# Windowed attention into a rational feed-forward layer on one Trainium2 core: chunks of 512 tokens, the division by remainder, and no GpSimd in the loop

## The chip, the cores and the metric

The program runs on one core of one Trainium2 chip. The core has a matrix engine (TensorE, PE in the profile, with its weight loads listed apart as PEld), VectorE (DVE), ScalarE (ACT), GpSimd (POOL), a queue that issues transfers (SyncE, SP), and 16 DMA engines. Operands lie in SBUF; matmuls write to PSUM, eight banks of 512 float32 columns on each of 128 partitions. The metric is the device time of one execution in microseconds, lower is better.

## The reference

Attention over 8 batches and 8 heads of 576 positions and 64 dimensions, each position seeing itself and the 63 before it; then a feed-forward layer on all 4608 tokens of width 512, with a rational function between its two matrices (512 x 2048 and 2048 x 512).

```python
scores = scale * np.matmul(q, k.transpose(0, 1, 3, 2))
rel = pos[:, None] - pos[None, :]
scores = np.where((rel >= 0) & (rel < 64), scores, -1000000000.0)
attn = np.exp(scores - np.max(scores, axis=-1, keepdims=True))
attn = attn / (np.sum(attn, axis=-1, keepdims=True) + 1e-09)
attn_out = np.matmul(attn, v)
x = attn_out.transpose(0, 2, 1, 3).reshape(B * S, H * D)
h = x @ w_in
P = a[0] + a[1] * h + a[2] * h**2 + a[3] * h**3
Q = 1.0 + np.abs(b[0]) * np.abs(h) + np.abs(b[1]) * h**2
out = (P / (Q + 1e-6)) @ w_out
```

The two weight matrices are handed over as 64-bit floats; the others as 32-bit.

## The kernel before

The tokens are cut into chunks of `CH` = 384. For each chunk the attention is computed in four **units**, one for each pair of heads (`hp`); a unit yields one 128 x 384 block of x, stored transposed as a rounded part `xh` and a remainder `xl`. The feed-forward layer then runs in **steps** (c, i): chunk c and block i of the 16 blocks of 128 hidden columns.

A step has three parts. `ffn1` (L234) makes one PSUM bank h of 128 hidden columns by 384 tokens with 12 matmuls: for each of four 128-row blocks of x the products of high weight and low x, high and high, low weight and high x. Then comes the **gate**, P divided by Q: ScalarE takes |h| and the first linear form of P; VectorE finishes P but for a[0]; the denominator is formed in `u`, for the first `DEC` = 28 gates by ScalarE (L250) and VectorE (L251), for the other 164 by GpSimd (L253, L254); ScalarE makes the reciprocal as exp(-ln u); VectorE improves it by one Newton step (L258, L259), multiplies (L260), ScalarE rounds the result to `gh` (L263) and VectorE takes the remainder `gl` (L264). `ffn2` (L274) adds the step's share of the output with 9 matmuls, three for each of the three 128-token tiles, into PSUM banks that stay open for the chunk's 16 steps. ffn2 of a step is written `LAG` = 3 steps behind its ffn1.

The order of steps: the first half of chunk 0 (8 steps), all 16 of chunk 1, the second half of chunk 0, and then chunk by chunk. So each weight block is decoded once and used soon after. The output of chunk 0's first half is kept in SBUF (`part`) and added at its end.

Weight decoding (`decode`, L101) turns 512 x 128 64-bit floats into two float32 parts. A transfer fills `w_st`; ScalarE takes the magnitude of the upper words, VectorE limits it, shifts it and merges in three bits of the lower word and the sign (L114 to L118); ScalarE rounds to the high part (L121), VectorE subtracts for the low part (L122). There are 32 decodings, all of them within the first 32 steps.

An attention unit has four parts. `unit_load` (L142) issues q, k and v; where a batch ends inside the chunk each of these is issued twice. `unit_scores` (L172): per 64-position tile and head one matmul of 64 x 128 scores into a PSUM tile of two banks; VectorE scales and masks (L188, L192) and takes the maximum; ScalarE exponentiates and sums; VectorE divides, from chunk 2 on GpSimd multiplies by the reciprocal sum (L205). `unit_transpose` (L208) transposes on TensorE into the same two-bank buffer and ScalarE copies out. `unit_av` (L217) multiplies by v into a third bank and ScalarE and VectorE store `xh`, `xl`. The units of the next chunk are spread over the steps before it, one every four steps, `AHEAD` = 3 steps early.

PSUM: two banks for h, two for scores and transposes, one for av, three for the output. Scratch tiles of the gate have two buffers each, `gh` and `gl` LAG + 1. The framework sets the semaphores, and orders each engine's instructions by its own estimate of their times; each engine then works its list in order, SP its transfers.

Of the kernel before, what the change touches and what calls it, by code (L numbers as in the profile page):

```python
# [31 lines left out]
def swa_rational_ffn(ctx: ExitStack, tc: tile.TileContext, qT, kT, v, w_in, w_out, a, b, out):  # L32
    nc = tc.nc
    P = 128
    B, HP, _, S = qT.shape
# [57 lines left out]

    wi_h = const.tile([P, NCC, DFF], F32R, name="wi_h")
    wi_l = const.tile([P, NCC, DFF], F32R, name="wi_l")
# [2 lines left out]
    w_in_v = w_in.rearrange("(cc p) f -> p cc f", p=P)
    w_out_v = w_out.rearrange("(fc p) e -> p fc e", p=P)

    def decode(src, hi, lo):  # L101

        w = stage.tile([P, 512, 2], U32, name="w_st", bufs=2)
        if len(src.shape) == 3:
            nc.sync.dma_start(out=w.rearrange("p (c n) two -> p c (n two)", c=src.shape[1]), in_=src)
        else:
            nc.sync.dma_start(out=w.rearrange("p n two -> p (n two)"), in_=src)
        low, high = w[:, :, 0], w[:, :, 1]
        c = stage.tile([P, 512], U32, name="w_c")
        cf = c.bitcast(F32)  # L110


        nc.scalar.activation(cf, w.bitcast(F32)[:, :, 1], AF.Abs)
        nc.vector.tensor_scalar(out=cf, in0=cf, scalar1=2.0 ** -15, scalar2=None, op0=ALU.max)  # L114
# [3 lines left out]
        nc.vector.scalar_tensor_tensor(out=c, in0=high, scalar=0xC0000000, in1=c, op0=ALU.bitwise_and, op1=ALU.bitwise_or)  # L118
        if len(hi.shape) == 3:
            cf = cf.rearrange("p (c n) -> p c n", c=hi.shape[1])  # L120
        nc.scalar.copy(out=hi, in_=cf)  # L121
        nc.vector.tensor_tensor(out=lo, in0=cf, in1=hi.bitcast(F32), op=ALU.subtract)  # L122
# [10 lines left out]

    def segments(c):

        g, left = c * TC, TC
        while left:
            n = min(left, TPB - g % TPB)
            yield g // TPB, g % TPB, n
            g, left = g + n, left - n  # L140

    def unit_load(c, hp):  # L142
# [3 lines left out]
        row = v.shape[2]  # L146
        kw, vw, first = [], [], None
        j = kb = vb = 0
        for bi, t0, n in segments(c):
            nc.sync.dma_start(out=q[:, j:j + n, :].rearrange("p t s -> p (t s)"),  # L150
                              in_=qT[bi, hp, :, t0 * WIN:(t0 + n) * WIN])
            k0 = max(t0 - 1, 0)
            nw = n if t0 else n - 1
            nc.sync.dma_start(out=kt[:, kb:kb + nw + 1, :].rearrange("p t s -> p (t s)"),
                              in_=kT[bi, hp, :, k0 * WIN:(k0 + nw + 1) * WIN])
            nc.sync.dma_start(out=vt[:, vb:vb + nw, :],
                              in_=bass.AP(v.tensor, (bi * S + k0 * WIN) * row + hp * P,
                                          [[row, P], [WIN * row, nw], [1, P]]))
            for t in range(t0, t0 + n):
                if t == 0:  # L160
                    first = j
                w = max(t - 1, 0) - k0
                kw.append(kb + w)
                vw.append(vb + w)
                j += 1
            kb += nw + 1
            vb += nw
# [225 lines left out]
```

## Time and profile before

| | |
|---|---|
| median of 3 runs | 1039.95 us |
| lowest run | 1039.42 us |
| span of the profiled execution | 1038.0 us |
| TensorE busy | 954.8 us, 92% |
| VectorE busy | 896.2 us, 86% |
| ScalarE busy | 706.8 us, 68% |
| GpSimd busy | 383.4 us, 37% |
| moved by DMA | 64.08 MB, 62 GB/s |

The three runs are 1039.42, 3231.52 and 1039.95 us; the second is an outlier that the median leaves out. The span runs from the first instruction of the profiled execution to its last and lies 2.0 us under the median; the page gives no other time for that execution.

How to read it: the busy shares of two engines are close, so the totals don't say which one sets the time. They are averages over stretches in which different work goes on, and have to be taken apart by time. A matmul's listed duration includes its run through the array and overlaps the next one's; the pace of TensorE is the distance between starts.

### The profile page before, as it was taken

How to read it: one execution, taken by the hardware profiler on the slowest of the kernel's cores; microseconds unless marked ns; L12 is line 12 of the kernel's file. 1: busy time of each engine (PE TensorE's matmuls, PEld its weight loads, DVE VectorE, ACT ScalarE, POOL GpSimd, SP SyncE). 2: the span in 40 equal slices, each digit the busy share in tenths (PEclk: the TensorE clock that was granted, in tenths of full speed). 3: DMA queues.
4: the chain of work that ended last, by engine and by line, in shares of the span. 5: the costliest groups of instructions: out<-in, count | busy, mean ns of one | idle time of the engine just before them, and what ended most of it. 6: DMA issues, size and time to landing. Idle time of an engine off the chain costs nothing.

```text
span 1038.0 us, 18200 instructions
## 1 busy us (share of the span) xinstructions
PE 954.8 (92%) x6624; PEld 839.2 (81%) x6624; DVE 896.2 (86%) x1639; ACT 706.8 (68%) x1762; POOL 383.4 (37%) x395
## 2 busy tenths in 40 slices
PE   2677686999999999999999999999999999999997
PEld 2566565789888889888888888888888898888996
DVE  5999899988888888888888888888888888888885
ACT  4687767677676666666676676766766766766664
POOL 2000002004554543543543544544544444445332
PEclk9889789999999999999999999999999999999999
DMA  6744433121111111111112112111112112100000
GB/s 188 203 124 129 125 105 92 41 72 32 59 43 47 60 49 46 64 40 48 59 33 57 60 30 64 64 31 57 59 30 60 60 31 64 63 16 2 31 1 30
DMA packets 68536, 64.08 MB, mean 62 GB/s; under 512 B 4448, under 2 KB 61792, under 8 KB 68448
## 3 DMA queue, kind: packets, MB, share of 16 engines
q1 hardware_dynamic: 68448, 62.93, 19.8%
q8 instruction: 52, 0.85, 0.4%
q14 instruction: 36, 0.29, 0.1%
HBM read 53.48 MB, written 9.44 MB: 61 GB/s over the span
## 4 chain that ended last, share of the span: by engine, by line
DVE 33%; PE 22%; ACT 20%; POOL 16%; issue 5%; DMA 3%; POOLq 0%; SPq 0%; DVEq 0%; ACTq 0%
PE o L284 11%; PE h L239 9%; ACT sm L201 8%; POOL u L253 6%; DVE u L258 6%; POOL u L254 5%; POOL sm L205 5%; DVE nmx L198 4%; DVE u L259 3%; DVE gl L264 3%; DMA w_st<-w_in 3%; DVE num L247 2%; ACT ah L256 2%; DVE num L260 2%; DVE num L246 2%
## 5 line engine op out<-in xcount | busy, mean ns | idle before, releaser
L239 PE MATMUL h<-xl,wi_h 128*128 128x384 f32 x768 | 266.4, 347 | 24.6 <-DVE num L247 18.0
L239 PE MATMUL h<-xh,wi_h 128*128 128x384 f32 x768 | 261.5, 341 | 0.0
L239 PE MATMUL h<-xh,wi_l 128*128 128x384 f32 x768 | 260.8, 340 | 0.0
L284 PE MATMUL o<-wo_h,gl 128*128 128x512 f32 x576 | 236.7, 411 | 25.4 <-DVE gl L264 25.3
L253 POOL TENSOR_SCALAR u<-ah,b_sb 128x384 f32<-128x384 f32 x164 | 134.8, 825 | 284.2 <-ACT ah L244 172.4
L284 PE MATMUL o<-wo_h,gh 128*128 128x512 f32 x576 | 229.4, 398 | 0.0
L284 PE MATMUL o<-wo_l,gh 128*128 128x512 f32 x576 | 228.4, 397 | 0.0
L205 POOL TENSOR_TENSOR sm<-sm,rs 128x768 f32<-128x768 f32 x40 | 72.6, 1814 | 347.0 <-DVE rs L204 202.1
L264 DVE TENSOR_TENSOR gl<-num,gh 128x384 fp32r<-128x384 f32 x192 | 165.1, 864 | 15.0 <-ACT gh L263 11.9
L201 ACT ACTIVATE sm<-sm,nmx 128x128 f32<-128x128 f32 x288 | 111.8, 390 | 94.4 <-DVE nmx L198 94.2
L254 POOL TENSOR_TENSOR u<-u,ah 128x384 f32<-128x384 f32 x164 | 171.6, 1053 | 8.3
L239 PEld LDWEIGHTS h<-xl,wi_h 128*128 128x128 f32 x768 | 146.5, 191 | 33.1 <-DVE num L247 20.9
L284 PEld LDWEIGHTS o<-wo_h,gl 128*128 128x128 f32 x576 | 110.1, 191 | 57.9 <-DVE gl L264 32.1
L245 ACT ACTIVATE num<-h,a_sb 128x384 f32<-128x384 f32 x192 | 128.7, 670 | 35.3 <-DVE gl L264 35.2
L239 PEld LDWEIGHTS h<-xh,wi_h 128*128 128x128 f32 x768 | 146.6, 191 | 4.5
L256 ACT ACTIVATE ah<-u 128x384 f32<-128x384 f32 x192 | 100.3, 522 | 72.3 <-POOL u L254 70.4
L239 PEld LDWEIGHTS h<-xh,wi_l 128*128 128x128 f32 x768 | 146.5, 191 | 0.0
L258 DVE SCALAR_TENSOR_TENSOR u<-u,ah 128x384 f32<-128x384 f32 x192 | 111.1, 579 | 36.0 <-ACT ah L257 35.8
L284 PEld LDWEIGHTS o<-wo_h,gh 128*128 128x128 f32 x576 | 110.1, 191 | 24.9
L284 PEld LDWEIGHTS o<-wo_l,gh 128*128 128x128 f32 x576 | 110.3, 191 | 19.5
L246 DVE TENSOR_TENSOR num<-num,h 128x384 f32<-128x384 f32 x192 | 105.0, 547 | 21.9 <-ACT num L245 21.8
L263 ACT CAST gh<-num 128x384 fp32r<-128x384 f32 x192 | 96.7, 508 | 36.6 <-DVE num L260 36.6
(47 smaller groups left out, 1239.8 us busy)
## 6 DMA issues: line engine op xcount, KB each, us to landing
out<-ob SPq DMA_DIRECT2D x33, 256.0 KB, 2.0
w_st<-w_in SPq DMA_DIRECT2D x16, 512.0 KB, 4.1
w_st<-w_out SPq DMA_DIRECT2D x16, 512.0 KB, 3.7
q<-qT SPq DMA_DIRECT2D x32, 192.0 KB, 3.2
vt<-v SPq DMA_DIRECT2D x16, 384.0 KB, 3.4
vt<-v SPq DMA_DIRECT2D x16, 320.0 KB, 3.5
kt<-kT SPq DMA_DIRECT2D x16, 224.0 KB, 3.6
kt<-kT SPq DMA_DIRECT2D x16, 192.0 KB, 3.4
```

The costliest lines, as they stand in the source:

```text
L201: nc.scalar.activation(sm[:, j, :], sm[:, j, :], AF.Exp, bias=nmx[:, j:j + 1], accum_out=sums[:, j:j + 1])
L205: (nc.vector if c < 2 else nc.gpsimd).tensor_tensor(out=sm, in0=sm, in1=rs.unsqueeze(2).broadcast_to([P, NR, P]), op=ALU.mult)
L239: nc.tensor.matmul(h, w[:, cc, i * P:(i + 1) * P], x[c, cc], start=n == 0, stop=n == 3 * NCC - 1)
L245: nc.scalar.activation(num, h, AF.Identity, scale=a_sb[:, 3:4], bias=a_sb[:, 2:3])
L246: nc.vector.tensor_tensor(out=num, in0=num, in1=h, op=ALU.mult)
L253: nc.gpsimd.tensor_scalar(out=u, in0=ah, scalar1=b_sb[:, 1:2], scalar2=b_sb[:, 0:1], op0=ALU.mult, op1=ALU.add)
L254: nc.gpsimd.tensor_tensor(out=u, in0=u, in1=ah, op=ALU.mult)
L256: nc.scalar.activation(ah, u, AF.Ln, bias=QADD)
L258: nc.vector.scalar_tensor_tensor(out=u, in0=u, scalar=QADD, in1=ah, op0=ALU.add, op1=ALU.mult)
L263: nc.scalar.copy(out=gh, in_=num)
L264: nc.vector.tensor_tensor(out=gl, in0=num, in1=gh.bitcast(F32), op=ALU.subtract)
L284: nc.tensor.matmul(acc[c][t], g[:, ts], w[:, i, :], start=first and n == 0, stop=last and n == 2)
```

## The change

Tokens: `CH` = 512, nine chunks instead of twelve, the steps 144 instead of 192, four output tiles instead of three, 12 matmuls in `ffn2`. The inputs are laid out over all batches in a row, so that a unit's q, k and v are one transfer each (in chunk 0 the first k and v tile come apart). Where a batch begins inside a chunk, the mask is one for all tiles and the tile's older half is overwritten by a memset.

Attention uses single banks: two buffers of one bank serve scores, transposes and av. The transposed tiles pass the output buffers' ring (`ob`, two slots).

The gate no longer uses GpSimd. It has no Newton step: with r = exp(-ln Q) the high part is the rounded P r, the remainder is (P - Q gh) r.

Decoding works in place in `w_st`, with one VectorE operation less; ScalarE scales the upper word by 2^-112 instead of taking its magnitude. The weight arrays are laid out by block.

`LAG` is 2. Chunk 0's partial sum goes to DRAM and comes back.

```diff
-CH = 384
+CH = 512
-DEC = 28
-LAG = 3
+LAG = 2
...
+    dram = ctx.enter_context(tc.tile_pool(name="dram", bufs=1, space=bass.MemoryType.DRAM))
-    ps_a = ctx.enter_context(tc.tile_pool(name="ps_a", bufs=3, space=bass.MemoryType.PSUM))
+    ps_a = ctx.enter_context(tc.tile_pool(name="ps_a", bufs=2, space=bass.MemoryType.PSUM))
...
-        nc.scalar.activation(cf, w.bitcast(F32)[:, :, 1], AF.Abs)
-        nc.vector.tensor_scalar(out=cf, in0=cf, scalar1=2.0 ** -15, scalar2=None, op0=ALU.max)
-        nc.vector.tensor_scalar(out=c, in0=c, scalar1=3, scalar2=0x3FFFFFF8, op0=ALU.logical_shift_left, op1=ALU.bitwise_and)
-        nc.vector.scalar_tensor_tensor(out=c, in0=low, scalar=29, in1=c, op0=ALU.logical_shift_right, op1=ALU.bitwise_or)
-        nc.vector.scalar_tensor_tensor(out=c, in0=high, scalar=0xC0000000, in1=c, op0=ALU.bitwise_and, op1=ALU.bitwise_or)
-        nc.scalar.copy(out=hi, in_=cf)
-        nc.vector.tensor_tensor(out=lo, in0=cf, in1=hi.bitcast(F32), op=ALU.subtract)
+        w = stage.tile([P, 1024], F32, name="w_st")
+        nc.sync.dma_start(out=w.bitcast(U32), in_=src)
+        w = w.rearrange("p (n two) -> p n two", two=2)
+        wu = w.bitcast(U32)
+        low, high = wu[:, :, 0], wu[:, :, 1]
+        nc.scalar.activation(w[:, :, 1], w[:, :, 1], AF.Copy, scale=2.0 ** -112)
+        nc.vector.tensor_scalar(out=low, in0=low, scalar1=29, scalar2=None, op0=ALU.logical_shift_right)
+        nc.vector.scalar_tensor_tensor(out=low, in0=high, scalar=0x80000000, in1=low, op0=ALU.bitwise_and, op1=ALU.bitwise_or)
+        nc.vector.scalar_tensor_tensor(out=low, in0=high, scalar=3, in1=low, op0=ALU.logical_shift_left, op1=ALU.bitwise_or)
+        c = w[:, :, 0]
+        nc.scalar.copy(out=hi, in_=c)
+        nc.vector.tensor_tensor(out=lo, in0=c, in1=hi.bitcast(F32), op=ALU.subtract)
...
+        nc.sync.dma_start(out=q.rearrange("p t s -> p (t s)"), in_=qT[hp, :, g * WIN:(g + TC) * WIN])
+        lo = 0 if g else 1
+        if lo:
+            nc.sync.dma_start(out=kt[:, 0, :], in_=kT[hp, :, 0:WIN])
+            for e in range(2):
+                nc.sync.dma_start(out=vt[e * 64:e * 64 + 64, 0, :], in_=v[0:WIN, hp * P:(hp + 1) * P])
+        nc.sync.dma_start(out=kt[:, lo:, :].rearrange("p t s -> p (t s)"), in_=kT[hp, :, (g + lo - 1) * WIN:(g + TC) * WIN])
+        nc.sync.dma_start(out=vt[:, lo:, :], in_=bass.AP(v.tensor, (g + lo - 1) * WIN * row + hp * P,
+                                                          [[row, P], [WIN * row, TC - lo], [1, P]]))
...
+        ps = [bank(), bank()]
...
+            nc.vector.scalar_tensor_tensor(out=sm[:, z * PR:(z + 1) * PR, :], in0=ps[z].rearrange("p (r c) -> p r c", c=P),
+                                           scalar=SCALE, in1=mask.unsqueeze(1).broadcast_to([P, PR, P]), op0=ALU.mult, op1=ALU.min)
+        for j in u["first"]:
+            e = j % 2
+            nc.vector.memset(sm.rearrange("p (z r) c -> p z r c", z=2)[e * 64:e * 64 + 64, :, j // 2, 0:WIN], NEG)
...
-        (nc.vector if c < 2 else nc.gpsimd).tensor_tensor(out=sm, in0=sm, in1=rs.unsqueeze(2).broadcast_to([P, NR, P]), op=ALU.mult)
+        nc.vector.tensor_tensor(out=sm, in0=sm, in1=rs.unsqueeze(2).broadcast_to([P, NR, P]), op=ALU.mult)
...
+        for z in range(2):
+            pT = op.tile([P, CH], F32, name="pT", tag="ob")
+            ps = bank()
+            for p in range(PR):
+                nc.tensor.transpose(ps[:, p * P:(p + 1) * P], u["sm"][:, z * PR + p, :], ident)
+            nc.scalar.copy(out=pT, in_=ps)
...
-        n_gates[0] += 1
-        if n_gates[0] <= DEC:
-            nc.scalar.activation(u, ah, AF.Identity, scale=b_sb[:, 1:2], bias=b_sb[:, 0:1])
-            nc.vector.tensor_tensor(out=u, in0=u, in1=ah, op=ALU.mult)
-        else:
-            nc.gpsimd.tensor_scalar(out=u, in0=ah, scalar1=b_sb[:, 1:2], scalar2=b_sb[:, 0:1], op0=ALU.mult, op1=ALU.add)
-            nc.gpsimd.tensor_tensor(out=u, in0=u, in1=ah, op=ALU.mult)
-        nc.scalar.activation(ah, u, AF.Ln, bias=QADD)
-        nc.scalar.activation(ah, ah, AF.Exp, scale=-1.0)
-        nc.vector.scalar_tensor_tensor(out=u, in0=u, scalar=QADD, in1=ah, op0=ALU.add, op1=ALU.mult)
-        nc.vector.scalar_tensor_tensor(out=u, in0=u, scalar=2.0, in1=ah, op0=ALU.subtract, op1=ALU.mult, reverse0=True)
-        nc.vector.scalar_tensor_tensor(out=num, in0=num, scalar=a_sb[:, 0:1], in1=u, op0=ALU.add, op1=ALU.mult)
-        nc.scalar.copy(out=gh, in_=num)
-        nc.vector.tensor_tensor(out=gl, in0=num, in1=gh.bitcast(F32), op=ALU.subtract)
+        nc.scalar.activation(u, r, AF.Identity, scale=b_sb[:, 1:2], bias=b_sb[:, 0:1])
+        nc.vector.tensor_tensor(out=u, in0=u, in1=r, op=ALU.mult)
+        nc.scalar.activation(r, u, AF.Ln, bias=QADD)
+        nc.scalar.activation(r, r, AF.Exp, scale=-1.0)
+        nc.vector.scalar_tensor_tensor(out=gh, in0=num, scalar=a_sb[:, 0:1], in1=r, op0=ALU.add, op1=ALU.mult)
+        nc.vector.scalar_tensor_tensor(out=u, in0=u, scalar=QADD, in1=gh.bitcast(F32), op0=ALU.add, op1=ALU.mult)
+        nc.vector.scalar_tensor_tensor(out=u, in0=num, scalar=a_sb[:, 0:1], in1=u, op0=ALU.add, op1=ALU.subtract)
+        nc.vector.tensor_tensor(out=gl, in0=u, in1=r, op=ALU.mult)
...
-            part[c] = const.tile([P, NTS, DO], F32, name="part")
+            part[c] = dram.tile([NTS, P, DO], F32, name="part")
             for t in range(NTS):
-                nc.scalar.copy(out=part[c][:, t, :], in_=o[t])
+                ob = op.tile([P, DO], F32, name="ob", tag="ob")
+                nc.scalar.copy(out=ob, in_=o[t])
+                nc.sync.dma_start(out=part[c][t], in_=ob)
...
+            pool, tag = (op, "ob") if s < total - 1 or t < 2 else (tmp, ("r", "u")[t - 2])
+            ob = pool.tile([P, DO], F32, name="ob", tag=tag)
             if c in part:
-                nc.vector.tensor_tensor(out=ob, in0=o[t], in1=part[c][:, t, :], op=ALU.add)
+                nc.sync.dma_start(out=ob, in_=part[c][t])
+                nc.vector.tensor_tensor(out=ob, in0=o[t], in1=ob, op=ALU.add)
...
+        if k >= 2:
+            unit_av(0, k - 2)
         if 1 <= k <= NU:
             unit_transpose(0, k - 1)
-        if k >= 2:
-            unit_av(0, k - 2)
```

More of the change, by code (lines that the diff above doesn't have):

```diff
@@ L91, in swa_rational_ffn @@
     make_identity(nc, ident)
[L94 to L95 removed]
+    wi_h = const.tile([P, NF, NCC, P], F32R, name="wi_h")
+    wi_l = const.tile([P, NF, NCC, P], F32R, name="wi_l")
     wo_h = const.tile([P, NF, DO], F32R, name="wo_h")
     wo_l = const.tile([P, NF, DO], F32R, name="wo_l")
[L98 to L99 removed]
     def decode(src, hi, lo):
[L103 to L122 removed]
@@ L124, in load_w_in @@
+        nc.vector.scalar_tensor_tensor(out=low, in0=high, scalar=3, in1=low, op0=ALU.logical_shift_left, op1=ALU.bitwise_or)
+        c = w[:, :, 0]
+        nc.scalar.copy(out=hi, in_=c)
+        nc.vector.tensor_tensor(out=lo, in0=c, in1=hi.bitcast(F32), op=ALU.subtract)
     def load_w_in(i):
-        sl = slice(i * P, (i + 1) * P)
-        decode(w_in_v[:, :, 2 * i * P:2 * (i + 1) * P], wi_h[:, :, sl], wi_l[:, :, sl])
+        f = "p c n -> p (c n)"
+        decode(w_in[i], wi_h[:, i].rearrange(f), wi_l[:, i].rearrange(f))
@@ L128, in load_w_out @@
     def load_w_out(i):
-        decode(w_out_v[:, i, :], wo_h[:, i, :], wo_l[:, i, :])
+        decode(w_out[i], wo_h[:, i, :], wo_l[:, i, :])
     xh, xl = {}, {}
     live = {}
[L134 to L140, printed above, removed]
     def unit_load(c, hp):
@@ L145, in unit_load, with bank @@
         vt = kv.tile([P, TC, P], F32, name="vt")
[L146 to L167, printed above, removed]
-        m0 = None if first is None else MASKS[first]
-        live[c, hp] = dict(q=q, kt=kt, vt=vt, kw=kw, vw=vw, m0=m0)
+        row = v.shape[1]
+        g = c * TC
+        nc.sync.dma_start(out=q.rearrange("p t s -> p (t s)"), in_=qT[hp, :, g * WIN:(g + TC) * WIN])
[7 more added lines that the diff above has]
+                                                          [[row, P], [WIN * row, TC - lo], [1, P]]))
+        live[c, hp] = dict(q=q, kt=kt, vt=vt, first=[j for j in range(TC) if (g + j) % TPB == 0])
+    def bank():
+        return ps_a.tile([P, 512], F32, name="ps", tag="ps")
     def unit_scores(c, hp):
         u = live[c, hp]
-        ps = ps_a.tile([P, 2, 512], F32, name="ps_s", bufs=1)
+        ps = [bank(), bank()]
         for p in range(PR):
@@ L209, in unit_transpose @@
         u = live[c, hp]
-        ps = ps_a.tile([P, 2, 512], F32, name="ps_s", bufs=1)
-        for j in range(2 * PR):
-            nc.tensor.transpose(ps[:, j // PR, (j % PR) * P:(j % PR + 1) * P], u["sm"][:, j, :], ident)
-        pT = att.tile([P, 2, PR * P], F32, name="pT", bufs=1)
-        nc.scalar.copy(out=pT, in_=ps[:, :, 0:PR * P])
-        u["pT"] = pT
+        u["pT"] = []
+        for z in range(2):
[4 more added lines that the diff above has]
+            nc.scalar.copy(out=pT, in_=ps)
+            u["pT"].append(pT)
     def unit_av(c, hp):
         u = live.pop((c, hp))
-        ps = ps_a.tile([P, TC, WIN], F32, name="ps_x", bufs=1)
+        ps = bank()
         for j in range(TC):
             for z in range(2):
-                nc.tensor.matmul(ps[z * 64:z * 64 + 64, j, :], u["vt"][:, u["vw"][j], z * 64:z * 64 + 64],
-                                 u["pT"][:, z, j * WIN:(j + 1) * WIN], start=True, stop=True)
+                nc.tensor.matmul(ps[z * 64:z * 64 + 64, j * WIN:(j + 1) * WIN], u["vt"][:, j, z * 64:z * 64 + 64],
+                                 u["pT"][z][:, j * WIN:(j + 1) * WIN], start=True, stop=True)
         xh[c, hp] = xp.tile([P, CH], F32R, name=f"xh{hp}")
         xl[c, hp] = xp.tile([P, CH], F32R, name=f"xl{hp}")
-        x = ps.rearrange("p t s -> p (t s)")
-        nc.scalar.copy(out=xh[c, hp], in_=x)
-        nc.vector.tensor_tensor(out=xl[c, hp], in0=x, in1=xh[c, hp].bitcast(F32), op=ALU.subtract)
+        nc.scalar.copy(out=xh[c, hp], in_=ps)
+        nc.vector.tensor_tensor(out=xl[c, hp], in0=ps, in1=xh[c, hp].bitcast(F32), op=ALU.subtract)
     gs = {}
-    n_gates = [0]
     def ffn1(c, i):
```

70 lines of the change are left out of this document (28 added, 42 removed).

## The prediction

> **What bounds the kernel now.** I read the row of slices on the page first, then windows over the two stages that it shows, then the timeline of each stage's busiest engine. Two slice rows:
>
> ```profile
> PE   2677686999999999999999999999999999999997
> DVE  5999899988888888888888888888888888888885
> ```
>
> A slice is 26 us. TensorE is full from the eighth on, VectorE before that. Windows make it exact (columns: length, then busy time of PE, weight loads, VectorE, ScalarE, GpSimd):
>
> ```profile
> 0.00:252.66 252.66, 187.23 (x1318) 157.75 (x1319) 228.47 (x455) 175.18 (x426) 24.43 (x39) 0.91 0.38 113
> 20.00:200.00 180.00, 130.49 (x913) 109.34 (x914) 171.25 (x345) 125.95 (x308) 8.38 (x3) 0.88 0.42 124
> 60.00:100.00 40.00, 33.80 (x252) 28.05 (x251) 40.00 (x85) 30.65 (x72) 0.00 (x0) 0.91 0.43 128
> 200.00:252.66 52.66, 52.11 (x353) 44.90 (x352) 47.20 (x91) 40.21 (x89) 9.17 (x9) 1.00 0.15 47
> 357.00:971.00 614.00, 603.90 (x4291) 536.47 (x4292) 529.54 (x937) 423.64 (x1077) 287.87 (x283) 1.00 0.15 47
> ```
>
> So there are two stages. The **head** (weight decoding, the 32 steps of chunks 0 and 1) is VectorE's: 171.25 of 180 us, and all of 60 to 100. The **steady part** is TensorE's: 603.90 of 614. At 252.66 the 33rd step starts, and I cut there. TensorE's timeline gives its beat:
>
> ```profile
> 252.66 0.34 PE L239 MATMUL h<-xl,wi_h 128*128 128x384 f32 x1
> ...
> 282.80 0.38 PE L212 MATMUL ps_s<-ident,sm 128*128 128x128 f32 x2
> ...
> 301.97 0.49 PE L212 MATMUL ps_s<-ident,sm 128*128 128x128 f32 x3
> ...
> 357.04 0.50 PE L284 MATMUL o<-wo_h,gl 128*128 128x512 f32 x1 [1.50 <-DVE gl L264]
> ...
> 959.39 0.34 PE L239 MATMUL h<-xl,wi_h 128*128 128x384 f32 x1
> ...
> 988.56 0.40 PE L284 MATMUL o<-wo_h,gl 128*128 128x512 f32 x1
> ...
> 992.70 0.34 PE L239 MATMUL h<-xl,wi_h 128*128 128x384 f32 x1
> ...
> 996.88 0.40 PE L284 MATMUL o<-wo_h,gl 128*128 128x512 f32 x1
> ...
> 1033.99 0.40 PE L284 MATMUL o<-wo_h,gh 128*128 128x512 f32 x1
> ```
>
> 988.56 to 992.70 holds 18 matmuls of 512 columns, 0.230 us each; from there to 996.88 are 24 of 384, 0.174 each. A step is 12 x 0.174 + 9 x 0.230 = 4.16. Four steps with one attention unit take 301.97 - 282.80 = 19.17, so a unit costs TensorE 19.17 - 16.64 = 2.53. A chunk takes (959.39 - 252.66) / 9 = 78.53, of which 16 x 4.16 + 4 x 2.53 = 76.7 is work and 1.5 the wait at the chunk's edge (357.04).
>
> VectorE's beat in the saturated stretch: instructions start closer together than they last.
>
> ```profile
> 65.97 0.96 DVE L205 TENSOR_TENSOR sm<-sm,rs 128x768 f32<-128x768 f32 x1
> 66.84 0.43 DVE L114 TENSOR_SCALAR w_c<-w_c 128x512 f32<-128x512 f32 x1
> 67.18 0.56 DVE L264 TENSOR_TENSOR gl<-num,gh 128x384 fp32r<-128x384 f32 x1
> 67.65 0.56 DVE L251 TENSOR_TENSOR u<-u,ah 128x384 f32<-128x384 f32 x1
> ...
> 72.05 0.70 DVE L118 SCALAR_TENSOR_TENSOR w_c<-w_st,w_c 128x512 uint32<-128x512 uint32 x1
> 72.65 0.62 DVE L247 SCALAR_TENSOR_TENSOR num<-num,a_sb,h 128x384 f32<-128x384 f32 x1
> 73.17 0.57 DVE L258 SCALAR_TENSOR_TENSOR u<-u,ah 128x384 f32<-128x384 f32 x1
> ```
>
> I take spacings as prices: 0.87 for 768 elements, 0.34 for the one-input form on 512, 0.47 for two inputs on 384, 0.60 on 512, 0.52 with a coefficient column on 384. So 128 elements more cost 0.13, and the coefficient form on 512 is 0.65, the multiply on 1024 elements 1.13. Other rows, less the same 0.09:
>
> ```profile
> L264 DVE TENSOR_TENSOR gl<-num,gh 128x384 fp32r<-128x384 f32 x192 | 165.1, 864 | 15.0 <-ACT gh L263 11.9
> L198 DVE TENSOR_REDUCE nmx<-sm 128x6 f32<-128x768 f32 x48 | 45.4, 947 | 0.0
> L203 DVE TENSOR_SCALAR sums<-sums 128x6 f32<-128x6 f32 x48 | 8.2, 171 | 31.6 <-ACT sm L201 31.6
> L192 DVE SCALAR_TENSOR_TENSOR sm<-ps_s,mask 128x384 f32<-128x384 f32 x64 | 32.5, 550 | 0.0
> L205 POOL TENSOR_TENSOR sm<-sm,rs 128x768 f32<-128x768 f32 x40 | 72.6, 1814 | 347.0 <-DVE rs L204 202.1
> ```
>
> L264 averages 0.86 against 0.56 in the stretch where GpSimd was idle (0.00 above). That surcharge goes with GpSimd; TensorE hides it today.
>
> **The change, part by part.**
>
> *Chunks of 512, TensorE.* Steps fall from 192 to 144, each 24 x 0.230 = 5.52. All FFN matmuls: 192 x 4.16 = 799 before, 144 x 5.52 = 795 after. Units fall from 48 to 36, each 4/3 of 2.53 = 3.37: unchanged in sum. A chunk: 16 x 5.52 + 4 x 3.37 + 1.5 = 103.3, where 512 tokens cost 78.53 x 4/3 = 104.7 before. The gain is 1.4 per chunk.
>
> *VectorE per gate.* Seven operations, four at 0.60 and three at 0.65: 4.35 for 512 tokens, against 5 x 0.47 + 2 x 0.52 = 3.39 for 384 while GpSimd had no part. Per unit: two masks 1.20, maximum 1.12, two small ones of L203's form 0.18, multiply 1.13 (GpSimd's before, from chunk 2 on), xl 0.60, and 32 memsets over 36 units: 4.3. A memset is bounded by 0.08 (L203's form) and 0.47; it is tiny, so 0.1. Before: 2 x 0.46 + 0.86 + 0.18 + 0.87 + 0.47 = 3.3. A steady chunk then asks 16 x 4.35 + 4 x 4.3 = 87 us of VectorE under 103.3 of TensorE: 84%, hidden if dependent operations are interleaved as now. If each ran at its whole duration plus the 0.02 between, it would be about 99: still under.
>
> *Decoding.* One operation less: 0.34 + 3 x 0.60 = 2.14 against 2 x 0.34 + 3 x 0.60 = 2.48. The shift now reads and writes every second word, which no row shows; bounds 0.34 and 0.60, and I take 0.34, the row of the same form. The two-input forms read such a stride already in L118. The Trainium skill, VectorE: DVE Perf Modes, "What auto-detection actually checks", names no unit stride for the fast one-source form of 32-bit data; by it the shift stays short, and no run here shows it.
>
> *The head.* Up to the cut VectorE does 32 decodings, 31 gates, 12 units. Before: 79.4 + 105.1 + 39.6, less what GpSimd took, 4.9: 219. After: 68.5 + 134.9 + 51.6 = 255. The 36 more, at the 95% busy of 20 to 200, move the cut by 38 to 291. Between 200 and 252.66 VectorE had 5.5 idle, so 285 is the low end; a long shift adds 32 x 0.26 / 0.95 = 9. TensorE's work up to there, 61 halves of a step at 2.76 and 12 units at 3.37, is 209 and stays below.
>
> *ScalarE.* It gains the denominator's scaling (from GpSimd) and loses the cast of gh.
>
> ```profile
> L244 ACT ACTIVATE ah<-h 128x384 f32<-128x384 f32 x192 | 93.2, 485 | 35.6 <-PE h L239 33.2 <-DVE u L259 1.4 <-PE ps_s L212 0.8
> L245 ACT ACTIVATE num<-h,a_sb 128x384 f32<-128x384 f32 x192 | 128.7, 670 | 35.3 <-DVE gl L264 35.2
> L250 ACT ACTIVATE u<-ah,b_sb 128x384 f32<-128x384 f32 x28 | 19.7, 708 | 0.0
> L256 ACT ACTIVATE ah<-u 128x384 f32<-128x384 f32 x192 | 100.3, 522 | 72.3 <-POOL u L254 70.4 <-DVE u L251 1.5
> L257 ACT ACTIVATE ah<-ah 128x384 f32<-128x384 f32 x192 | 101.1, 527 | 3.8
> L201 ACT ACTIVATE sm<-sm,nmx 128x128 f32<-128x128 f32 x288 | 111.8, 390 | 94.4 <-DVE nmx L198 94.2
> L228 ACT CAST xh<-ps_x 128x384 fp32r<-128x384 f32 x48 | 22.4, 468 | 2.8 <-PE ps_x L223 2.8
> L298 ACT COPY ob<-o 128x512 f32<-128x512 f32 x30 | 17.4, 580 | 2.7 <-PE o L284 1.4 <-DMA out<-ob 1.3
> ```
>
> 128 elements add 0.11 (L298 against L228): 0.60 + 0.78 + 0.82 + 0.63 + 0.64 = 3.5 a step, with exponentials and copies under 5 of 6.4: hidden.
>
> *Slack of a gate (LAG 2).* Its chain: 3.5 on ScalarE, 0.69 + 0.75 + 0.69 + 0.75 + 0.69 on VectorE, some 0.5 of hand-overs: 7.5. Between ffn1 and its ffn2 TensorE has four halves, 11.0, so 3.5 are left. Before, LAG 3 gave six halves of 2.08: 12.5 for shorter instructions. The wait at the edge (357.04) is of this kind; I keep its 1.5 per chunk, bounds 0 and 1.5 + 2.8 (rival 2). Behind a late ffn2 TensorE's whole queue stands, the next ffn1 first.
>
> *DMA and SP.*
>
> ```profile
> out<-ob SPq DMA_DIRECT2D x33, 256.0 KB, 2.0
> w_st<-w_in SPq DMA_DIRECT2D x16, 512.0 KB, 4.1
> w_st<-w_out SPq DMA_DIRECT2D x16, 512.0 KB, 3.7
> SPq L156 <- PE ps_x L223: 510.5, 44, 19.3
> ```
>
> Unit loads shrink from four issues to three; SP idles 510.5 us behind the v loads, so this is worth 0. The weights' new layout makes w_in like w_out, 0.4 sooner, under VectorE's queue. Chunk 0's partial sum goes to DRAM and back: four stores and four loads join SP's queue, loads and copies behind them. At step 33 each of two slots passes load, add, store (2.0 + 0.7 + 2.0) before its second use; the next chunk's ffn2 waits between 0 and 5, and I take 2. Masks (16 selects fewer on GpSimd), av ahead of the transposes in the prologue: 0, since the first weights' landing covers them.
>
> *Sum.* Last chunk and end: before 1033.99 + 0.40 - 959.39 = 75.0, of which 66.6 beat and 8.4 drain; after 88.3 + 8.7 = 97. From the last matmul to the span's end 3.6. So 291 + 2 + 6 x 103.3 + 97 + 3.6 = 1013.4, against the span of 1038.0; the median lies 2.0 above that span, so 1015.4, called **1016**, 2.3% under the median. Its own range is 1003 to 1030.
>
> **The rivals.**
> 1. *Slower: attention eats the gate's slack.* At each unit VectorE takes 4.3 us (2.4 before, the multiply being GpSimd's) and ScalarE eight exponentials of 0.39, in front of a gate with 3.5 to spare; if both fall into one chain, 3.9 are lost. With 24 units after the cut that is 1016 + 94 = 1110. It decides from 1.9 a unit on (45 us). For it: the edge already waits on gl. Against: VectorE's 16% idle lets the gate catch up.
> 2. *The two-slot ring and single banks.* Four output copies and each unit's two transposed tiles pass the same two slots; the third copy waits for a landing of 2.0. At most 2.8 at the edge and 0.7 (a copy) per unit: 5.6 x 7 = 39; half of it gives 1036.
> 3. *The head is heavier.* The long shift adds 9, and staging tiles held to the last subtraction, 1.3 longer, starve a decoding: up to 32 x 1.3 / 2 = 21. Middle: 1033.
> 4. *No overlap on VectorE.* Every operation of 255 us in the head pays its duration, 0.09 more on some 440 instructions: 40 us, 1056. Against: starts 67.18 and 67.65 with 0.56 each. The Trainium skill, same page, "The DRAIN you can't avoid", says that the next operation cannot issue before the pipe is empty; by that rule this is the time, and the trace does not bear it out.
> 5. *Better:* no wait at the edges, the head at 285: 1016 - 10 - 8 = 998.
>
> **How the numbers follow.** Forecast 0.52, two thirds of it under 1019; rivals 1 to 5: 0.12, 0.14, 0.12, 0.03, 0.07. Two per cent, 20.8 us, is about what this measurement tells apart. Faster: 0.35 + 0.07 = 0.42. Slower: 0.12. Same: 0.46. Range 1002 to 1052: it leaves out rival 1 and some 0.07 of rivals 4 and 5.
>
> **What would show it.** The 33rd step near 291 with VectorE full before; 512-column matmuls in L239's place 0.230 apart; chunks of 103 to 104; VectorE near 85 to 90% busy, with no instruction stretched; the shift at 0.43. Wrong if TensorE waits for gl or h more than once a chunk, if chunks pass 107, or the cut lies past 305.

## The result, and the profile after

The changed kernel takes 1058.18 us (median of 4 runs, 1057.24 to 1058.55) against 1039.68 for the kernel before (a fourth run of it took 1038.65): a ratio of 1.0176, interval 1.0160 to 1.0191. It is slower, though by less than 2%, where 1016 us and a gain of 2.3% were forecast, and it lies 6 us above the range. The profiled execution spans 1056.3 us, 42.9 more than the 1013.4 of the forecast's sum.

The page of the changed kernel, its busy times and the slices (26 us each):

```profile
PE 985.2 (93%) x6048; PEld 786.5 (74%) x6048; DVE 903.3 (86%) x1424; ACT 675.0 (64%) x1506; POOL 2.1 (0%) x11
...
PE   2769768899998999999999999999999999999998
...
DVE  5789968999887988888888888888889888888886
...
PEclk9899978999999999999999999999999999999999
```

TensorE is full from the ninth slice on, but for the thirteenth. In the first eight, VectorE, which was to be full there, is at 9 only three times. Windows, the first from the start of the span to step 33, the others cut at the first feed-forward matmul of steps 1, 17, 33, 41 and 113 (columns: length, then busy time of PE, weight loads, VectorE, ScalarE, GpSimd, then PEclk, DMA share, GB/s):

```profile
0.00:308.76 308.76, 248.58 (x1576) 194.74 (x1577) 264.16 (x440) 198.29 (x458) 2.07 (x11) 0.93 0.35 109
...
36.02:209.35 173.33, 136.32 (x928) 104.22 (x926) 152.35 (x263) 116.55 (x277) 0.00 (x0) 0.88 0.43 135
209.35:308.76 99.41, 98.82 (x509) 79.14 (x508) 88.59 (x138) 64.45 (x128) 0.00 (x0) 1.00 0.09 28
308.76:369.46 60.70, 55.03 (x391) 43.55 (x390) 50.94 (x81) 33.51 (x78) 0.00 (x0) 1.00 0.29 87
369.46:848.89 479.43, 479.43 (x3026) 385.52 (x3024) 417.80 (x649) 315.58 (x718) 0.00 (x0) 1.00 0.16 51
```

The same two halves of the head in the kernel before:

```profile
29.30:171.13 141.83, 103.19 (x750) 85.79 (x750) 135.45 (x273) 104.02 (x263) 3.18 (x2) 0.86 0.45 133
171.13:252.66 81.53, 74.87 (x460) 64.79 (x461) 74.75 (x147) 57.80 (x125) 14.37 (x10) 0.98 0.16 50
```

Three places hold nearly all of the 42.9 us.

- **The head**: the 33rd step starts at 308.76 instead of 291, +17.8. Its second half (steps 17 to 32) is TensorE's: 98.82 busy of 99.41 us. In the first half neither engine is full: VectorE idles 21.0 of 173.33 us, in the kernel before 6.4 of 141.83.
- **The eight steps from the 33rd**: 60.70 us, of which TensorE is idle 5.7, where eight steady steps take 479.43 / 9 = 53.27. That is +7.4; 2 were allowed for.
- **The steady part**: 106.5 us a chunk (16 steps) instead of 103.3, with no idle TensorE at all; six chunks make +19.4.

The rest is small: up to step 129 the remaining steps give back 2.2, and the last chunk with the end takes 103.1 instead of 100.6. Sum: 17.8 + 5.4 + 19.4 - 2.2 + 2.5 = 42.9.

In the steady part one row of TensorE's timeline shows where it goes. The unit that runs there (columns: start, length, then the instruction and its count):

```profile
490.87 1.15 PE L182 MATMUL ps<-pT,vt 128*64 128x64 f32 x32
491.95 1.09 PE L145 MATMUL ps<-kt,q 64*64 64x128 f32 x16
...
498.91 1.09 PE L145 MATMUL ps<-kt,q 64*64 64x128 f32 x16
```

and the kernel before:

```profile
386.26 0.89 PE L182 MATMUL ps_s<-kt,q 64*64 64x128 f32 x24
```

Before, a unit's 24 score instructions (two for each matmul) stood together, the two heads in turn, and took 0.89 us. Now there are 32 in two groups, one for each head, 7 us apart, and **each group of 16 takes 1.09 us, as long as 32 in alternation do** (1.10, e1 below). Four instructions start every 0.109 us while the heads alternate, two with one head alone. The Trainium skill, TensorE: Matmul & The Clock Gate, "The mechanism" (Part 3), says that matmuls on different parts of the array overlap; the trace agrees (32 in 1.10 us), and adds that the two heads' matmuls overlap only where they stand next to each other in the queue (16 alone take 1.09).

The groups of the changed kernel (columns: count, then busy time and mean ns) that answer to the prediction's prices:

```profile
L145 PE MATMUL ps<-kt,q 64*64 64x128 f32 x1152 | 79.5, 291 | 13.4 <-DMA kt<-kT 6.1 <-DVE sm L149 4.5 <-DVE xl L187 1.6
...
L99 DVE TENSOR_SCALAR w_st<-w_st 128x512 uint32<-128x512 uint32 x32 | 13.5, 423 | 26.1 <-DMA w_st<-w_in 17.3 <-DMA w_st<-w_out 8.4
...
L216 DVE TENSOR_TENSOR gl<-u,r 128x512 fp32r<-128x512 f32 x144 | 98.6, 685 | 1.2
```

The strided shift stayed short (0.423), and with GpSimd out of the loop gl averages 0.685 (L216), close to the 0.69 that the prediction's chain has for it. Scores are busy for 79.5 us; before it was 47.0 for as many instructions.

### The profile page after: what moved, and what is told of

It reads as the page before. It is cut to its first block, busy times and chain, and to the rows that moved or that the text cites. A ratio compares the mean times of both kernels' runs of the same rounds, so it can differ in the third digit from the quotient of the medians.

```text
span 1056.3 us, 15824 instructions
## 1 busy us (share of the span) xinstructions
PE 985.2 (93%) x6048; PEld 786.5 (74%) x6048; DVE 903.3 (86%) x1424; ACT 675.0 (64%) x1506; POOL 2.1 (0%) x11
## 4 chain that ended last, share of the span: by engine, by line
PE 79%; DVE 11%; DMA 6%; ACT 3%; SPq 1%; issue 1%; ACTq 0%; DVEq 0%
PE o L236 35%; PE h L196 34%; PE ps L145 5%; DMA w_st<-w_in 4%; PE ps L182 3%; PE ps L173 2%; DMA w_st<-w_out 2%; ACT sm L159 1%; DVE w_st L100 1%; DVE w_st L101 1%; DVE gh L213 1%; DVE nmx L156 1%; DVE wi_l L104 1%; DVE num L206 1%; DVE u L208 1%
## 5 line engine op out<-in xcount | busy, mean ns | idle before, releaser
L196 PE MATMUL h<-xl,wi_h 128*128 128x512 f32 x576 | 235.1, 408 | 14.1 <-DVE num L207 11.4
L196 PE MATMUL h<-xh,wi_h 128*128 128x512 f32 x576 | 231.7, 402 | 0.0
L196 PE MATMUL h<-xh,wi_l 128*128 128x512 f32 x576 | 230.5, 400 | 0.0
L206 DVE TENSOR_TENSOR num<-num,h 128x512 f32<-128x512 f32 x144 | 98.5, 684 | 39.1 <-ACT num L204 38.0
L205 ACT ACTIVATE u<-r,b_sb 128x512 f32<-128x512 f32 x144 | 117.5, 816 | 0.0
L204 ACT ACTIVATE num<-h,a_sb 128x512 f32<-128x512 f32 x144 | 111.8, 776 | 0.0
L213 DVE SCALAR_TENSOR_TENSOR gh<-num,a_sb,r 128x512 fp32r<-128x512 f32 x144 | 107.3, 746 | 2.8 <-ACT r L211 2.6
L215 DVE SCALAR_TENSOR_TENSOR u<-num,a_sb,u 128x512 f32<-128x512 f32 x144 | 107.5, 747 | 1.4
L207 DVE SCALAR_TENSOR_TENSOR num<-num,a_sb,h 128x512 f32<-128x512 f32 x144 | 106.8, 741 | 0.5
L208 DVE TENSOR_TENSOR u<-u,r 128x512 f32<-128x512 f32 x144 | 98.8, 686 | 3.1 <-ACT u L205 2.3
```

The costliest lines, as they stand in the source:

```text
L196: nc.tensor.matmul(h, w[:, i, cc, :], x[c, cc], start=n == 0, stop=n == 3 * NCC - 1)
L204: nc.scalar.activation(num, h, AF.Identity, scale=a_sb[:, 3:4], bias=a_sb[:, 2:3])
L205: nc.scalar.activation(u, r, AF.Identity, scale=b_sb[:, 1:2], bias=b_sb[:, 0:1])
L206: nc.vector.tensor_tensor(out=num, in0=num, in1=h, op=ALU.mult)
L207: nc.vector.scalar_tensor_tensor(out=num, in0=num, scalar=a_sb[:, 1:2], in1=h, op0=ALU.add, op1=ALU.mult)
L208: nc.vector.tensor_tensor(out=u, in0=u, in1=r, op=ALU.mult)
```

## The experiments

Each was compared with the kernel before on the same chip; intervals are 95%. "Steps 33 to 40" stands for the eight steps from the 33rd.

### Are separated heads the steady loss?

**e1_two_bank_tile.** One PSUM tile of two banks instead of two single ones, so that both heads' scores can only run together.

```diff
-    def bank():
-        return ps_a.tile([P, 512], F32, name="ps", tag="ps")
+    def banks():
+        t = ps_a.tile([P, 2, 512], F32, name="ps", tag="ps", bufs=1)
+        return t[:, 0, :], t[:, 1, :]
```

> The changed kernel with one PSUM tile of two banks for scores, transposes and av in place of two single banks; all else as in it. Theory A (TensorE does the scores of the two heads one after the other, because the second bank is not yet free when the first is): a unit's 32 score instructions stand together again and take about 1.1 us instead of 2 x 1.02, a steady chunk falls from 106.5 to 102.7 us, and the time falls by 24 units x 0.95 plus a little in the head, to 1030 to 1036 us. Rival B (the unit is longer for another reason: more switches, longer drains of 512 columns): chunk and time stay within 3 us of 1058. Rival C (one slot of two banks holds transposes and av up): TensorE waits inside chunks, 1058 or more.

1140.70 us, ratio 1.0978 (1.0961 to 1.0996). Its TensorE timeline (in brackets the idle time before, and what ended it):

```profile
583.19 1.10 PE L146 MATMUL ps<-kt,q 64*64 64x128 f32 x32 [1.41 <-DVE xl L189]
...
589.06 0.80 PE L198 MATMUL h<-xl,wi_h 128*128 128x512 f32 x1 [3.18 <-DVE num L209]
...
600.22 1.15 PE L184 MATMUL ps<-pT,vt 128*64 128x64 f32 x32 [2.19 <-ACT pT L176]
```

Together, 32 instructions take 1.10: the price is confirmed. But with one slot the scores wait for the subtraction that reads x, av waits for the copy of the transposed tiles, and TensorE stands still: the other way of losing time was far dearer.

**e2_before_heads_in_turn.** The kernel before, with the loop over heads outside.

```diff
-        for p in range(PR):
-            for z in range(2):
+        for z in range(2):
+            for p in range(PR):
```

> The kernel before, with the score matmuls of one head issued ahead of those of the other; nothing else. Theory A: its 24 score instructions of a unit take 24 x 0.064 = 1.5 us instead of 0.82, a chunk 81.3 instead of 78.5, and with 36 units behind the cut the time rises by about 26 us, to 1063 to 1070. Rival B: within 3 us of 1040.

1044.18 us, ratio 1.0046 (1.0029 to 1.0062). The unit's group:

```profile
389.41 1.15 PE L182 MATMUL ps_s<-kt,q 64*64 64x128 f32 x24
```

1.15 instead of 0.89: the effect is there in the kernel before too, but well under the size expected (0.26 us a unit instead of 0.7, and 4.8 us in all instead of 26). In this group the starts of the single instructions show the second head's first matmuls between the first head's last ones; nothing else stands between the heads there. In the changed kernel seven us of other work do.

**e5_scores_together.** The changed kernel; both heads' first matmuls are issued first, the other 14 behind them, in every chunk.

```diff
+        first = score(0, 0, 0)
+        with tc.issue_after(first.ins):
+            second = score(0, 1, 0)
+        with tc.issue_after(second.ins):
+            ...
```

> The changed kernel with one thing altered: the issue order of a unit's scores is forced, so that both heads' first matmuls are issued, in this order, ahead of the 14 others. The two single banks stay. Theory A (a head issued alone runs 2 score instructions every 0.109 us, two heads alternating run 4): a unit's scores take 1.0 to 1.2 us in place of 2 x 1.02, four steady steps take 25.7 in place of 26.64, a chunk 102.9 in place of 106.5; six chunks give 22, the head a little: about 1034 us. Rival (waiting for the later bank costs it back): TensorE stands some 1 us ahead of each unit's scores until the low half of x has read its bank; the chunk stays at 106 or more and the time at 1056 to 1065.

1065.40 us, ratio 1.0239 (1.0219 to 1.0259), slower than the change itself. The steady part did gain, 476.0 us for the 72 steps that took 479.4; it gained less than the 16 expected. In part this is because the very first matmul still ran alone (0.36 us to the next instruction) and only 30 instructions ran together: from start to next start, the scores of these 72 steps took 26.3 us instead of 36.8. Some 7 of these 10.5 us went again, of which TensorE's idle time, new here, is 1.9; the cause of the rest stays open. The larger loss is elsewhere: steps 33 to 40 took 75.2 us instead of 60.7. Forcing the order had made worse something that the theory did not contain; the next group shows what.

**e10_scores_together_after_xl.** From chunk 3 on, a unit's first score waits for the subtraction that reads the last bank, and the other 15 are issued behind it. Chunks 0 to 2 are left alone.

```diff
+        first = score(*order.pop(0))
+        if c > 2:
+            tc.add_manual_dep(first.ins, bank_read[-1].ins.name, ...)
+            with tc.issue_after(first.ins):
+                ...
```

> The changed kernel; from chunk 3 on a unit's first score waits for the subtraction that reads the last bank, and the other 15 are issued behind it, so that all 16 (32 instructions) stand together with the heads alternating; chunks 0 to 2 keep their order, so that no score there waits for a parked bank. Theory A: a unit's scores take 1.03 us in place of 2 x 1.02, four steady steps 25.6 in place of 26.64, a chunk 102.5; 24 units make 24 us: about 1034. The head stays as it is, the 33rd step at 308 to 310. Rival (waiting for both banks stops TensorE): PE shows idle time ahead of the scores, a chunk of 105 or more, and 1050 or more.

1048.66 us, ratio 1.0084 (1.0068 to 1.0100): 9.5 us better than the change, not 24. Its window over steps 41 to 112:

```profile
369.04:837.48 468.44, 464.06 (x3025) 370.53 (x3024) 415.33 (x648) 315.24 (x717) 0.00 (x0) 1.00 0.17 52
```

That is 104.1 us a chunk: between theory and rival. All 32 instructions stand together, but TensorE idles 4.4 us here, at the edges of chunks (waits for output copies, transposed tiles and h), where the changed kernel has none.

### What are steps 33 to 40 waiting for?

**e3_pt_in_sm.** The changed kernel with the transposed tiles written back over the scores, so that they leave the output buffers' ring; in the prologue av comes ahead of the next unit's scores.

```diff
-            pT = op.tile([P, CH], F32, name="pT", tag="ob")
+            pT = u["sm"][:, z * PR:(z + 1) * PR, :].rearrange("p r c -> p (r c)")
```

> The changed kernel with the transposed tiles written back into the score tile, so that the two-slot ring serves output copies alone (in the prologue av then comes ahead of the next unit's scores). Theory D (in the head TensorE and VectorE stand behind the ring: partial sum and transposed tiles wait for each other's slots, at about 135 to 160 us and at 320 to 340): 8 to 20 us less, 1038 to 1050. Rival E (the head is held by staging and VectorE's work alone): within 3 us of 1058. The steady chunk stays at 106.5 either way.

1069.72 us, ratio 1.029 (1.0263 to 1.0316). Steps 33 to 40 still take 60.4, and the head is 13 us longer. The shared ring isn't the cause of what these steps lose. (With e1's edit on top, e4_both: 1138.63 us, like e1.)

**e7_part_four_slots.** The third and fourth tile of chunk 0's partial sum pass through slots of the gate's temporaries.

```diff
-                ob = op.tile([P, DO], F32, name="ob", tag="ob")
+                pool, tag = (op, "ob") if t < 2 else (tmp, ("r", "u")[t - 2])
+                ob = pool.tile([P, DO], F32, name="ob", tag=tag)
```

> The changed kernel with the third and fourth tile of the first chunk's partial sum passing through slots of the gate's temporaries, at its store and at its return, in place of a second use of the two slots of the ring. Theory S (the second use of two slots is what waits): the eight steps from the 33rd take 55 to 57 us in place of 60.7, and the stall near 145 us shrinks; the time falls by 4 to 10 us, to about 1051. Rival (the round trip itself, or the gates whose temporaries are now taken, costs as much): these steps stay at 59 to 61 and the time within 3 us of 1058.

1065.26 us, ratio 1.0235 (1.0215 to 1.0254); steps 33 to 40 take 63.5. So the partial sum's second pass through two slots, for which the prediction allowed its 2 us, isn't what waits either.

The timeline of the changed kernel's attention up to there gives another cause. TensorE, with scores at L145, av at L182:

```profile
174.96 1.15 PE L182 MATMUL ps<-pT,vt 128*64 128x64 f32 x30 [0.16 <-ACT pT L174]
176.04 1.09 PE L145 MATMUL ps<-kt,q 64*64 64x128 f32 x16
...
180.05 1.09 PE L145 MATMUL ps<-kt,q 64*64 64x128 f32 x16
...
202.60 1.15 PE L182 MATMUL ps<-pT,vt 128*64 128x64 f32 x32 [0.68 <-ACT pT L174]
...
260.33 0.45 PE L145 MATMUL ps<-kt,q 64*64 64x128 f32 x8
```

ScalarE, the casts that read av's bank:

```profile
252.77 1.29 ACT L186 CAST xh<-ps 128x512 fp32r<-128x512 f32 x2 [1.50 <-PE h L196]
...
314.32 0.59 ACT L186 CAST xh<-ps 128x512 fp32r<-128x512 f32 x1 [3.75 <-PE ps L182]
```

Chunk 2's first two units have their av at 174.96 and 202.60, but x has two slots for each head pair, and chunks 0 and 1 hold both until chunk 1's last ffn1. So the results stay in PSUM, **one in each of the only two attention banks**, until 252.77; the second group of scores ends at 181, and none runs before 260. Two units are then left for the 48 us from there to the 33rd step, each goes through the same two banks at some 26 us, and the last x comes at 314.32, after that step has begun (308.76). Steps 33 and 34 do nine of their twelve ffn1 matmuls and wait with both h banks; the other three of each start at 321.05. ScalarE and VectorE get no h in that time, and TensorE pays afterwards. In the kernel before, av had a bank of its own beside the scores' two, and the last x of chunk 2 came at 250.26, ahead of 252.66.

In e5 a unit also needs both banks at once, so the second unit could not go on beside a parked result (its first matmul runs at 195.5, the next at 257.4): three units were left at 251, and the last x came at 329.7.

**e9_x0_three_slots.** A third slot for the first unit's x, chunk 2's units one step apart; paid for with one buffer of q and the reserve for dynamic transfers.

```diff
-        xh[c, hp] = xp.tile([P, CH], F32R, name=f"xh{hp}")
-        xl[c, hp] = xp.tile([P, CH], F32R, name=f"xl{hp}")
+        xh[c, hp] = xp.tile([P, CH], F32R, name=f"xh{hp}", bufs=3 if hp == 0 else 2)
+        xl[c, hp] = xp.tile([P, CH], F32R, name=f"xl{hp}", bufs=3 if hp == 0 else 2)
...
-            every = prev // NU
+            every = 1 if c == 2 else prev // NU
...
```

> The changed kernel with a third slot for the first unit's x (high and low, 4 KB a partition, paid for by one buffer of q instead of two and the reserve for dynamic DMAs) and chunk 2's four units placed one step apart instead of two. In the changed kernel two av results of chunk 2 stand in the only two attention banks from 174 and 203 us until chunk 1 lets go of its x at about 252, no score runs from 181 to 260, and the last unit's x is there at 315.6, after the 33rd step has begun at 308.8. Theory P (these parked banks make the last unit late, both gate banks stand half filled, and that is the loss of the eight steps from the 33rd): the last x of chunk 2 is there by 300, these eight steps take 53.3 to 56 us in place of 60.7, the time falls to about 1051 to 1053. Rival (the partial sum's return through two slots costs it): they stay at 59 to 61, the time within 3 us of 1058.

1053.22 us, ratio 1.0124 (1.0107 to 1.0140). ScalarE's casts for units 2 to 4 of chunk 2, and the window over steps 33 to 40:

```profile
251.08 1.07 ACT L186 CAST xh<-ps 128x512 fp32r<-128x512 f32 x2
...
277.69 0.57 ACT L186 CAST xh<-ps 128x512 fp32r<-128x512 f32 x1
```

```profile
310.97:362.19 51.22, 51.22 (x297) 40.14 (x296) 45.69 (x73) 31.98 (x76) 0.00 (x0) 1.00 0.23 74
```

The last x comes 33 us ahead, and the eight steps take 51.22 with TensorE full. The partial sum goes the same way through DRAM as before, so the rival falls. Of the 9.5 us that these steps gain, 5.7 are TensorE's idle time; the other 3.8 are attention that now runs elsewhere (297 instructions instead of 391), and the whole kernel gains 5.0. Where the last x stands against the 33rd step and what the eight steps take go together:

| kernel | 33rd step starts | last x of chunk 2 | steps 33 to 40 |
|---|---|---|---|
| e9 | 310.97 | 277.7 | 51.2 |
| changed | 308.76 | 314.3 | 60.7 |
| e7 | 312.38 | 318.8 | 63.5 |
| e5 | 306.02 | 329.7 | 75.2 |
| e8 | 302.16 | 325.8 | 75.2 |
| e11 | 308.67 | 277.0 | 49.7 |

In e3, e6, e10 and e12 the last x comes 3.5 to 6.4 us after the 33rd step has started, and the eight steps take 59.2 to 61.6.

### What sets the end of the head?

In the first half of the head VectorE now waits for staged weights. The waits of the changed kernel from 36 to 209 us (columns: us in all, times, longest):

```profile
DVE w_st L99 <- DMA w_st<-w_out: 8.4, 4, 2.6
DVE w_st L99 <- DMA w_st<-w_in: 6.7, 6, 2.1
```

The kernel before has no such wait there. **e6_early_release** frees a staging tile one step earlier; the new tile's room comes from the reserve for dynamic transfers.

```diff
+        c = stage.tile([P, 512], F32, name="w_c", bufs=1)
-        nc.vector.scalar_tensor_tensor(out=low, in0=high, scalar=3, ...)
-        c = w[:, :, 0]
+        nc.vector.scalar_tensor_tensor(out=c.bitcast(U32), in0=high, scalar=3, ...)
...
```

> The changed kernel with the last decoding step writing to a tile of its own (2 KB, one buffer), so that a staging tile is free after that step and not after the subtraction. Theory B (held staging slows the head): the two copies of the weights finish decoding at about 207 to 211 us in place of 216, the 33rd step starts at 300 to 304 in place of 308.8, the time falls by 5 to 9 us, to about 1051. Rival (VectorE, or the stall at the first chunk's partial sum, sets the pace of the head): the 33rd step moves by less than 3 us and the time stays within 3 us of 1058.

1059.89 us, ratio 1.0188 (1.0172 to 1.0204): no change. Its windows over both halves of the head:

```profile
36.00:211.16 175.16, 137.78 (x935) 105.56 (x935) 159.89 (x273) 117.58 (x280) 0.00 (x0) 0.89 0.40 129
211.16:307.29 96.13, 96.13 (x492) 76.44 (x491) 79.67 (x124) 59.14 (x119) 0.00 (x0) 1.00 0.11 34
```

Decoding now ends at 188.4 instead of 216.2, even sooner than expected, and VectorE does 7.5 us more in the first half. The end of the head moves by 1.5. What VectorE gains is of no use in the second half, where TensorE is busy 96.13 of 96.13 us.

**e12_two_products** leaves out, for chunks 0 and 1, the products of low weights by high values in both multiplications. That takes a third of TensorE's feed-forward work out of the head and leaves VectorE's instructions as they are.

```diff
-            for w, x in ((wi_h, xl), (wi_h, xh), (wi_l, xh)):
+            for w, x in ((wi_h, xl), (wi_h, xh), (wi_l, xh))[:2 if c < 2 else 3]:
...
-            for n, (g, w) in enumerate(((gl, wo_h), (gh, wo_l), (gh, wo_h))):
+            products = ((gl, wo_h), (gh, wo_h)) if c < 2 else ((gl, wo_h), (gh, wo_l), (gh, wo_h))
```

> The changed kernel with one of the three products of each feed-forward multiplication left out for chunks 0 and 1 (low weights by high values, in both multiplications): a third of TensorE's feed-forward work of the first 32 steps, 32 x 8 x 0.23 = 59 us; VectorE's work is the same. If VectorE sets the pace of the whole head, as the prediction had it, the 17th step stays at 205 to 211 and the 33rd at 303 to 309. If TensorE sets it from the 17th step on (98.8 busy of 99.4 us there in the changed kernel, VectorE 88.6), steps 17 to 32 fall from 99.4 to VectorE's own pace, 88.6 / 0.95 = 93, and the 33rd step comes 6 us or more sooner. If TensorE sets it everywhere, the 17th step too comes 15 us or more sooner than 209.

```profile
36.20:211.86 175.66, 121.64 (x819) 91.09 (x817) 156.64 (x268) 117.89 (x281) 0.00 (x0) 0.81 0.42 133
211.86:292.33 80.47, 69.95 (x361) 52.06 (x359) 77.79 (x124) 57.62 (x118) 0.00 (x0) 0.98 0.10 34
```

The 17th step comes no sooner, at 211.86 instead of 209.35, although TensorE now idles 54 us in the first half (its granted clock there is 0.81 instead of 0.88). Steps 17 to 32 fall from 99.41 to 80.47, and now VectorE is nearly full (77.79). So the first half is not TensorE's and the second is. The 33rd step starts at 292.33, 1.3 us from the 291 that were forecast from VectorE's work alone. That it comes so near is partly luck: VectorE had 258.0 us of work behind it by then, 6 less than in the changed kernel, and was 88% busy, not the 95% of the forecast. (1040.63 us, ratio 1.0011, 0.9999 to 1.0024.)

### Together

**e8_all_three** has the edits of e5, e6 and e7.

> The three edits together. If theories A, B and S hold and their parts add up: 1058 - 22 - 7 - 6 = about 1023 us, under the kernel before by 1.6%. If only A holds: about 1034, a chunk of 102.9, the 33rd step near 305. If none holds: 1055 to 1060.

1053.58 us, ratio 1.0128 (1.0111 to 1.0145): the 33rd step at 302.16, steps 33 to 40 at 75.2 as in e5, then 104.0 a chunk. The chunk was 105.8 in e5; neither of the other two edits is in the code of these steps, and why it fell further stays open.

**e11_both_late_fixes** has those of e9 and e10.

> Both edits together. If theories A and P hold and add up: 1058 - 24 - 6 = about 1028 us, 1.1% under the kernel before; what is left against the predicted 1016 is then the head (some 16 us). If only A holds about 1034, if only P holds about 1052.

**1024.44 us, ratio 0.9848 (0.9834 to 0.9863)**: 33.7 us better than the change, and faster than the kernel before by 1.5%. One unit's scores, and the windows over steps 33 to 40 and 41 to 112:

```profile
449.33 1.10 PE L144 MATMUL ps<-kt,q 64*64 64x128 f32 x32
```

```profile
308.67:358.38 49.71, 49.71 (x297) 39.48 (x296) 45.00 (x71) 31.31 (x73) 0.00 (x0) 1.00 0.24 77
358.38:819.88 461.50, 461.50 (x3026) 370.48 (x3024) 416.40 (x649) 314.86 (x718) 0.00 (x0) 1.00 0.17 52
```

A chunk takes 461.5 / 4.5 = 102.6, and TensorE has no idle time from the 33rd step up to the last chunk. The scores of these 72 steps take 18.6 us from start to next start, where the changed kernel's took 36.8: 18.2 less, and the steady part gains 17.9. Alone the two edits gave 5.0 and 9.5. Why they give more than that together is only partly seen: the idle time at the chunks' edges that e10 has is gone, but no run tells apart whether the sooner unit, the single buffer of q or the third slot did it.

## Why the prediction was wrong, step by step

- **The head's end (291, was 308.8).** VectorE's added work was priced well: 36 us more than before were forecast, and 264.2 - 228.5 = 35.7 came. (The 219 that the prediction adds up for the kernel before lies 9 under that page's 228.5, but only the difference entered the sum.) The step that failed is the sentence that TensorE's work up to there "is 209 and stays below". TensorE was busy 248.6 us up to there, partly at a lower clock (0.88 granted in steps 1 to 16; ffn2's matmuls start 0.43 apart near 170 us, where 0.53 was granted), and in steps 17 to 32 it sets the pace, 98.8 of 99.4 us. The sentence compares two totals; VectorE's added work lies in both halves (16.9 us in steps 1 to 16, 13.8 in 17 to 32), and in the second TensorE's longer steps are longer still. With TensorE relieved (e12) the head ends 16.4 us sooner. The cut past 305, one of the prediction's own signs of being wrong, came.
- **What stays open in the head.** The 95% that the forecast had for VectorE failed too: up to the 33rd step VectorE idles 44.6 us, where 291 leaves 26.5. Most of what is more than before lies in steps 1 to 16 (21.0 us, was 6.4). What sets the pace there is not known: neither less TensorE work (e12, 175.66 us) nor shorter waits for staged weights (e6, 175.16) shortened the 173.33.
- **The partial sum (+2, was +7.4).** The place was right, the cause wrong. The loss is chunk 2's last unit, late because av's results are parked in both attention banks (e9). The single banks had been looked at in rival 2, but for the chunk's edges in the steady part; the one spot where x has no free slot was not looked at.
- **A steady chunk (103.3, was 106.5), the largest part.** The step that failed is "unchanged in sum" for the units. It failed for one part of the unit: from start to next start the scores take 2 x 1.02 instead of 4/3 of 0.82 = 1.09. Four steps took 26.64 instead of 25.83: +0.95 for the scores, +0.12 for ffn1's matmuls (0.233 apart, not 0.230), -0.38 for the edge wait, which the forecast kept and which went away, and 0.1 that no row was found for. Rival 2 named the resource (single banks) with a price that would have fitted (20 us), but as waits for slots; TensorE never waited. Two banks in turn changed the *order* of issue: the second head's bank is the one that av has just filled, so that head comes later and alone. With the heads together (e11) a chunk takes 102.6, below the forecast.
- **The last chunk and the end (100.6, was 103.1).** Small, and its cause stays open; no unit's scores run there, so it is not the steady part's loss.
- **Rival 1, gates with LAG 2:** did not come. In the steady part nothing waits for gl, with one lag less and the multiply on VectorE.
- **Rival 3, a heavier head:** the staging wait is real (15.1 us), but shortening it alone is worth nothing (e6). (In e8, beside the edits of e5 and e7, the 33rd step comes 3.9 us sooner than in e5; no run shows which edit did it.) The long shift did not come: it took 0.423, which agrees with the Trainium skill, VectorE: DVE Perf Modes, "What auto-detection actually checks", where the fast one-source form has no condition on the stride.
- **Rival 4, no overlap on VectorE:** did not come; VectorE fills 77.79 of 80.47 us in e12, and operations of 0.69 start 0.60 apart as in the kernel before (L100 at 169.76, L101 at 170.36). The section that the prediction cites for it (the Trainium skill, VectorE: DVE Perf Modes, "The DRAIN you can't avoid") goes on to say that a next operation which is not held starts earlier; these spacings fit that.
- **Rival 5, better:** the waits at the edges did go away in the steady part, the shorter head did not come.

## What to carry to other kernels

Where two engines share a stretch, compare their work stage by stage: totals that fit can hide a stage in which the other engine is the bound. The larger work of each stage is still only a lower bound; steps 1 to 16 took 21 us more than the busier engine worked. When buffers are cut (three PSUM banks to two, a two-bank tile to single ones), ask not only who waits but what the new order of issue does to instructions that were fast because they stood side by side, and look for the one place in the schedule where a result cannot leave its buffer. An idle time that is plainly there, like VectorE's wait for staged weights, is worth nothing until the experiment that removes it moves the end.
